# wo loaded over all 128 partitions, with o brought to the matching layout by eight selection matmuls

## Chip, cores and metric

One core of a Trainium2 chip. The metric is the device time of one execution in microseconds. The kernel before takes 357.08 us (median of 3 runs, 356.75 to 357.36; 357.03 with the fourth run that was made beside the changed kernel). All runs quoted here are of the fast state; runs of one kernel agree within about 0.3%. A profile is of one execution; its span, from the first to the last instruction, is about 2 us shorter than the time of that execution, and the same event can lie some tenths of a microsecond apart in two profiles.

## The reference

A decode step: one token for each of two batches. Attention with 32 heads over a cache of 4096 keys, a small dense branch, and a gate between them. PV below is the product of the softmax weights with V; o is its result.

```python
# x [2,1,512]; k_cache, v_cache [2,32,4096,128]; wq [512,4096]; wo [4096,512], all bf16
g = sigmoid((x * gate_w).sum(-1, keepdims=True))
q = (x @ wq) by heads
scores = einsum("bhqd,bhkd->bhqk", q, k) * 128 ** -0.5
o = einsum("bhqk,bhkd->bhqd", softmax(scores), v)
a = o.reshape(B, 1, 4096) @ wo
b = relu(x @ w1) @ w2
return g * a + (1 - g) * b
```

K and V are 67 MB each, the weights 11 MB. Nothing is used twice, so the work is mostly a stream from HBM.

## The kernel before

SyncE issues all large loads in one queue, in the order wq, w1, w2, 16 K tiles, 16 V tiles, wo, four 4 MB slots in SBUF being used in turn. K and V tiles cover all 128 partitions. wo (4 MB) goes into slot 0 as soon as the thirteenth V tile has been used (`pv_12`), and so stands behind the last three V tiles in the queue. Its rows are (head h, 32-row group c of 128/32 = 4, row r). Partition 32c + h holds the 32 rows r of (h, c), so one transfer serves one c and 32 partitions:

```python
wo_in = A_wo.rearrange("(h c r) n -> c h r n", c=4, r=32)
...
WO_CUTS = (0, 16, 24, 28, 30, 32)          # five chunks of r: half, a quarter, an eighth, ...
for k in range(5):
    lo, hi = WO_CUTS[k], WO_CUTS[k + 1]
    for c in range(4):
        load(f"ld_wo_{k}_{c}", wo_sb[32 * c:32 * c + 32, lo:hi, :], wo_in[c, :, lo:hi, :],
             waits=["pv_12"] if k + c == 0 else [], sem=f"wo{k}")
```

After the last V tile, o (64 rows (b, h), 128 columns d = 32c + r) is scaled and moved to that layout by eight small matmuls in four column tiles of the array, and then projected, chunk by chunk of wo:

```python
def o_spread():
    # on_sb[(b,h), d] = o * (gate / softmax sum)
    for b in range(2):
        for c in range(4):
            matmul(bank(MISC, 32 * b, 32, 32 * c, 32 * c + 32), lhsT=ident16[0:64, 32 * b:32 * b + 32],
                   rhs=on_sb[:, 32 * c:32 * c + 32], start=True, stop=True, tile_position=(0, 32 * c), ...)
    # os_sb[p, r, b] <- bank(MISC)
def proj():
    for r in range(32):
        for c in range(4):                 # here c is a block of 128 output columns
            # at r in WO_CUTS: wait for that chunk of wo
            matmul(acc(c), lhsT=os_sb[:, r, :], rhs=wo_sb[:, r, 128 * c:128 * c + 128], start=(r == 0), stop=(r == 31), ...)
```

Of the kernel before, what the change touches and what calls it, by code (L numbers as in the profile page):

```python
# [4 lines left out]
ALU = mybir.AluOpType  # L5
# [134 lines left out]
def bass_gated_mix__gqa_block_cached__dense_activation_relu__decode_kernel(  # L140
# [12 lines left out]
    P = _Prog(nc)  # L153
    f32, b16 = dt.float32, dt.bfloat16
    sb = nc.alloc_sbuf_tensor
# [3 lines left out]
    ident16 = sb("ident16", [128, 128], b16)  # L159
    eye32 = sb("eye32", [128, 32, 32], b16)  # L160
    dmask = sb("dmask", [128, 4], b16)
    row3 = sb("row3", [128, 4, 4, 4], f32)
    rmask = sb("rmask", [128, 4], f32)
    sst = sb("sst", [128, PER, 64], f32)
    selb = sb("selb", [128, 124], f32)
    zt = sb("zt", [128, 512], b16)
    x_sb = sb("x_sb", [2, 512], b16)
    gw_sb = sb("gw_sb", [1, 512], b16)
# [25 lines left out]
    on_sb = sb("on_sb", [64, 128], b16)  # L194
# [6 lines left out]
    wo_sb = kv_sb[:, 0, :, :].rearrange("p r d -> p (r d)").rearrange("p (r n) -> p r n", r=32)  # L201
# [4 lines left out]
    def bank(b, c0, n, p0=0, p1=128):  # L206
        return PSF[p0:p1, 512 * b + c0:512 * b + c0 + n]
# [7 lines left out]
    O_BANK, MISC, ACC = 6, 7, 0  # L215

    def acc(c):
        return bank(ACC, 0, 128, 32 * c, 32 * c + 2)
# [4 lines left out]
    w2a_in = B_w2[0:1280, :].rearrange("(p t) n -> p t n", p=128)  # L223
    w2b_in = B_w2[1280:1376, :]
    wq_in = A_wq.rearrange("(p t) n -> p t n", p=128)
    wo_in = A_wo.rearrange("(h c r) n -> c h r n", c=4, r=32)
    out_ap = out.rearrange("b s d -> (b s) d")

    def kv_in(n):
# [5 lines left out]
    def load(name, dst, src, waits=(), eng="sp", sem=None):  # L235
        P.add(eng, lambda e: e.dma_start(dst, src), waits=waits, signal=name, sem=sem or name, inc=16)  # L236
# [7 lines left out]
    for n in range(32):  # L244
        waits = [{2: "f", 3: "qT"}[n]] if n in (2, 3) else []
# [4 lines left out]
    WO_CUTS = (0, 16, 24, 28, 30, 32)  # L250
    for k in range(5):
        lo, hi = WO_CUTS[k], WO_CUTS[k + 1]
        for c in range(4):
            load(f"ld_wo_{k}_{c}", wo_sb[32 * c:32 * c + 32, lo:hi, :], wo_in[c, :, lo:hi, :], waits=["pv_12"] if k + c == 0 else [],
                 sem=f"wo{k}")


    P.add("pool", lambda e: e.memset(ident16[:], 0.0), signal="c_i0")
# [1 line left out]
                                            compare_op=ALU.not_equal, fill=1.0, base=0, channel_multiplier=1),  # L260
          waits=["c_i0"], signal="c_id")
    P.add("pool", lambda e: e.memset(eye32[:], 0.0), waits=["c_id"], signal="c_e0")
    P.add("pool", lambda e: e.affine_select(out=eye32[:], in_=eye32[:], pattern=[[1, 32], [-1, 32]],
                                            compare_op=ALU.not_equal, fill=1.0, base=0, channel_multiplier=0),
          waits=["c_e0"], signal="c_eye")
    P.add("pool", lambda e: e.memset(row3[:], 0.0), waits=["c_eye"], signal="c_r0")
    P.add("pool", lambda e: e.affine_select(out=row3[:], in_=row3[:], pattern=[[-32, 4], [-4, 4], [-1, 4]],
                                            compare_op=ALU.not_equal, fill=1.0, base=0, channel_multiplier=1),
          waits=["c_r0"], signal="c_row3")
    P.add("pool", lambda e: e.memset(dmask[:], 0.0), waits=["c_row3"], signal="c_d0")  # L270
    for q in range(4):
        P.add("pool", lambda e, q=q: e.memset(dmask[32 * q:32 * q + 32, q:q + 1], 1.0), waits=["c_d0"] if q == 0 else [],
              signal="c_d" if q == 3 else None)
# [7 lines left out]
    for k in range(4):  # L281
        P.add("pe", lambda e, k=k: e.matmul(bank(k, 0, 512), lhsT=zt[:, 0:128], rhs=zt[:, :], start=True, stop=True),
              waits=["c_zt"] if k == 0 else [])
    for t in range(4):
        P.add("pe", lambda e, t=t: e.transpose(bank16(4, 2 * t, 2), x_sb[0:2, t:512:4], ident16[0:2, 0:2]),
              waits=["c_id", "ld_x"] if t == 0 else [], signal="xT" if t == 3 else None)
    for t in range(4):
        P.add("pe", lambda e, t=t: e.transpose(bank16(5, 2 * t, 1), gw_sb[0:1, t:512:4], ident16[0:1, 0:1]),  # L288
              waits=["ld_gw"] if t == 0 else [], signal="gwT" if t == 3 else None)
    P.add("dve", lambda e: e.tensor_copy(out=xT_sb[:, :, :], in_=bank16(4, 0, 8).rearrange("p (t b) -> p t b", t=4)),  # L290
          waits=["xT"], signal="xT_sb")
    P.add("dve", lambda e: e.tensor_copy(out=gwb_sb[:, :, :],
                                         in_=PSB[:, 5120:5128:2].unsqueeze(2).to_broadcast([128, 4, 128])),
          waits=["gwT"], signal="gwb")
    for t in range(4):
        P.add("pe", lambda e, t=t: e.matmul(bank(6, 0, 2), lhsT=gwb_sb[:, t, :], rhs=xT_sb[:, t, :],
                                            start=(t == 0), stop=(t == 3)),
              waits=["xT_sb", "gwb"] if t == 0 else [], signal="logit" if t == 3 else None)
    P.add("act", lambda e: e.activation(out=g_sb[:, :], in_=bank(6, 0, 2), func=ACT.Sigmoid), waits=["logit"], signal="g")
    P.add("dve", lambda e: e.tensor_scalar(out=gm_sb[:, :], in0=g_sb[:, :], scalar1=-1.0, scalar2=1.0, op0=ALU.mult, op1=ALU.add),  # L300
          waits=["g"], signal="gm")
    for h in range(HQ):
        for t in range(4):
            P.add("pe", lambda e, h=h, t=t: e.matmul(bank(7, 2 * h, 2), lhsT=wq_sb[:, t, h * 128:(h + 1) * 128],  # L304
                                                     rhs=xT_sb[:, t, :], start=(t == 0), stop=(t == 3)),
                  waits=["ld_wq"] if h + t == 0 else [], signal="qT" if h == HQ - 1 and t == 3 else None)
# [213 lines left out]
    def o_spread():  # L520
        P.add("dve", lambda e: e.tensor_scalar(out=on_sb[:, :], in0=bank(O_BANK, 0, 128, 0, 64), scalar1=rg[:, 0:1], scalar2=None,
                                               op0=ALU.mult), waits=["ov_15", "rg_0", "rg_1"], signal="on")
        for b in range(2):
            for c in range(4):
                P.add("pe", lambda e, b=b, c=c: e.matmul(
                    bank(MISC, 32 * b, 32, 32 * c, 32 * c + 32), lhsT=ident16[0:64, 32 * b:32 * b + 32],
                    rhs=on_sb[:, 32 * c:32 * c + 32], start=True, stop=True, tile_position=(0, 32 * c), skip_group_check=True),
                    waits=["on"] if b + c == 0 else [], signal="os" if (b, c) == (1, 3) else None)
        P.add("dve", lambda e: e.tensor_copy(out=os_sb[:, :, :].rearrange("p r b -> p b r"),
                                             in_=bank(MISC, 0, 64).rearrange("p (b r) -> p b r", b=2)),  # L530
              waits=["os"], signal="os_sb")

    def proj():
        for r in range(32):
            for c in range(4):
                w = ["os_sb"] if r == 0 else []
                if r in WO_CUTS:
                    w = w + [f"ld_wo_{WO_CUTS.index(r)}_{k}" for k in range(4)]
                P.add("pe", lambda e, r=r, c=c: e.matmul(acc(c), lhsT=os_sb[:, r, :], rhs=wo_sb[:, r, 128 * c:128 * c + 128],  # L539
                                                         start=(r == 0), stop=(r == 31), tile_position=(0, 32 * c), skip_group_check=True),  # L540
                      waits=w if c == 0 else [], signal="proj" if (r, c) == (31, 3) else None)
# [27 lines left out]
    for p in range(PER):  # L569
        v_sum(p, NIT - 1)  # L570
    stage_s()
    o_spread()
    proj()
    P.add("dve", lambda e: e.tensor_tensor(out=out_sb[:, :], in0=bank(ACC, 0, 128, 0, 98), in1=f_sb[:, :], op=ALU.add),  # L574
          waits=["proj"], signal="res")
    for b, eng in enumerate(("sp", "act")):
        P.add(eng, lambda e, b=b: e.dma_start(out_ap[b].rearrange("(c n) -> c n", c=4), out_sb[b:97 + b:32, :]), waits=["res"],
              signal=f"st_{b}", sem="st", inc=16)
# [51 lines left out]
```

## Time and profile before

| | before |
|---|---|
| time, median | 357.08 us |
| profiled span | 354.7 us |
| DMA rate while V loads | 433 GB/s |
| DMA rate while wo loads | 207 to 231 GB/s |
| start of the last PV batch (32 matmuls on the last V tile) | 334.99 us |
| end of the projection | 352.02 us |

Read it as one long transfer with a tail. As long as the loads set the end, time at which the DMA runs below its own best rate is lost, whatever "busy" says. The prediction below shows the lines. In them PE is TensorE (PEld its weight loads), DVE VectorE, ACT ScalarE, POOL GpSimd and SP SyncE. A stretch has its bounds, its length, the busy microseconds of PE, PEld, DVE, ACT and POOL with the number of instructions, then the granted TensorE clock (1.00 is full speed), the mean busy share of the 16 DMA engines, and GB/s. L478 is PV, L525 the selection of o, L529 the copy to os_sb, L539 the projection, L574 the final add; the change moves these to L481, L528, L532, L542, L577.

### The profile page before, as it was taken

What the parts mean: (1) busy time and instruction counts of PE and PEld (TensorE: products, weight loads), DVE (VectorE), ACT (ScalarE), POOL (GpSimd) and SP (SyncE); (2) the same over time, 40 slices, a digit from 0 to 9 for tenths busy, and PEclk for the clock granted to TensorE, in tenths of its full rate; (3) what the DMA queues carried; (4) which work ended last, traced back from release to release, by engine and by line L of the source; (5) the groups of instructions that cost most, each with busy time, mean ns of one, the idle gap of its engine ahead of it and who ended that gap; (6) DMA issues with size and microseconds to landing.
All of it is one profiled execution on the core that took longest, in us unless ns stands there. A gap on an engine that the chain in (4) does not pass through costs nothing.

```text
span 354.7 us, 8320 instructions
## 1 busy us (share of the span) xinstructions
PE 232.1 (65%) x3475; PEld 159.0 (45%) x3476; DVE 150.7 (42%) x285; ACT 99.9 (28%) x105; POOL 24.0 (7%) x47
## 2 busy tenths in 40 slices
PE   2535999999999999999993534444333344444242
PEld 0525887788777877788881111111111111111021
DVE  1012667666667666677669642111222222111020
ACT  1002666566565665576664000000000000000000
POOL 4030100111111111100000000000000000000000
PEclk9999999999999999999998586666555666555565
DMA  9999999999999999999999999999999999999994
GB/s 355 389 453 418 416 450 428 416 434 440 418 432 436 432 425 436 440 421 440 440 418 432 436 430 423 432 440 425 432 443 421 432 443 425 421 432 443 248 218 106
DMA packets 6146, 145.61 MB, mean 411 GB/s; under 512 B 915, under 2 KB 1014, under 8 KB 1398
## 3 DMA queue, kind: packets, MB, share of 16 engines
q1 hardware_dynamic: 6120, 145.43, 98.2%
q8 instruction: 9, 0.15, 0.2%
q14 instruction: 3, 0.02, 0.0%
q10 hardware_dynamic: 14, 0.00, 0.0%
HBM read 145.43 MB, written 0.00 MB: 410 GB/s over the span
## 4 chain that ended last, share of the span: by engine, by line
DMA 78%; PE 15%; SPq 3%; DVE 2%; issue 1%; DVEq 0%
DMA kv_sb<-in_A_k_cache_dram 35%; DMA kv_sb<-in_A_v_cache_dram 28%; DMA kv_sb<-in_A_wo_dram 10%; PE PS L353 8%; DMA kv_sb<-in_B_w_dram 5%; PE PS L478 4%; SPq L236 3%; PE PS L365 2%; DVE mt L419 1%; PE PS L330 0%; DVE ET_sb L432 0%; DVE pst L462 0%; DVE mT L421 0%; PE PS L539 0%; DVE mx L422 0%
## 5 line engine op out<-in xcount | busy, mean ns | idle before, releaser
L389 DVE COPY kt_sb<-PS 128x1024 bf16<-128x1024 bf16 x160 | 105.6, 688 | 58.4 <-PE PS L353 58.3
L353 PE MATMUL PS<-ident,kv_sb 128*128 128x128 bf16 x2048 | 122.9, 221 | 10.8 <-DMA kv_sb<-in_A_k_cache_dram 9.8
L353 PEld LDWEIGHTS PS<-ident,kv_sb 128*128 128x128 bf16 x2048 | 116.3, 99 | 25.0 <-issue 16.6
L386 ACT ACTIVATE kt_sb<-PS 128x1024 bf16<-128x1024 bf16 x96 | 94.5, 1022 | 72.4 <-PE PS L353 72.4
L478 PE MATMUL PS<-kv_sb,pst 128*16 128x512 bf16 x512 | 55.2, 608 | 59.8 <-issue 42.8
L478 PEld LDWEIGHTS PS<-kv_sb,pst 128*16 128x16 bf16 x512 | 16.5, 122 | 89.9 <-issue 89.2
L490 DVE TENSOR_SCALAR vo<-PS,rmask 128x128 f32<-128x128 f32 x16 | 5.6, 351 | 109.8 <-PE PS L478 109.8
L365 PE MATMUL PS<-kt_sb,qst 128*32 128x512 bf16 x512 | 34.2, 382 | 1.1 <-DVE kt_sb L389 1.1
L505 PE MATMUL PS<-vo,sst 128*64 128x128 f32 x32 | 8.4, 352 | 29.0 <-DVE vo L491 29.0
L399 POOL TENSOR_TENSOR qst<-q_sb,eye 128x512 bf16 x16 | 16.5, 1040 | 128.2 <-PE PS L365 116.5
L505 PEld LDWEIGHTS PS<-vo,sst 128*64 128x64 f32 x32 | 3.7, 165 | 42.5 <-issue 30.2
L491 DVE SCALAR_TENSOR_TENSOR vo<-PS,rmask,vo 128x128 f32<-128x128 f32 x48 | 16.8, 351 | 1.7
L365 PEld LDWEIGHTS PS<-kt_sb,qst 128*32 128x32 bf16 x512 | 10.9, 95 | 12.7 <-issue 3.3
L513 POOL COPY sst<-selb 128x64 f32 x16 | 3.6, 236 | 146.0 <-PE PS L505 146.0
L462 DVE TENSOR_TENSOR pst<-ET_sb,dmask 128x512 bf16<-128x512 bf16 x16 | 10.8, 684 | 0.1
L539 PE MATMUL PS<-kv_sb,os_sb 128*2 128x128 bf16 x128 | 4.3, 305 | 6.5 <-DMA kv_sb<-in_A_wo_dram 6.5
L539 PEld LDWEIGHTS PS<-kv_sb,os_sb 128*2 128x2 bf16 x128 | 2.9, 112 | 7.7 <-DMA kv_sb<-in_A_wo_dram 4.7
L304 PE MATMUL PS<-xT_sb,kv_sb 128*128 128x2 bf16 x128 | 3.6, 165 | 3.6 <-DMA kv_sb<-in_A_wq_dram 3.6
L304 PEld LDWEIGHTS PS<-xT_sb,kv_sb 128*128 128x128 bf16 x128 | 3.5, 104 | 3.7 <-DMA kv_sb<-in_A_wq_dram 3.7
L574 DVE TENSOR_TENSOR out_sb<-PS,f_sb 98x128 bf16<-98x128 f32 x1 | 0.3, 292 | 10.5 <-PE PS L539 10.5
L288 PE MATMUL PS<-ident,gw_sb 1*128 1x1 bf16 x4 | 0.3, 172 | 4.6 <-DMA gw_sb<-in_gate_w_dram 4.6
L307 DVE TENSOR_SCALAR q_sb<-PS 128x64 bf16<-128x64 f32 x1 | 0.2, 224 | 6.8 <-PE PS L304 6.8
(62 smaller groups left out, 35.9 us busy)
## 6 DMA issues: line engine op xcount, KB each, us to landing
kv_sb<-in_A_k_cache_dram SPq DMA_DIRECT2D x16, 4096.0 KB, 29.2
kv_sb<-in_A_v_cache_dram SPq DMA_DIRECT2D x16, 4096.0 KB, 35.1
kv_sb<-in_A_wq_dram SPq DMA_DIRECT2D x1, 4096.0 KB, 12.1
kv_sb<-in_A_wo_dram SPq DMA_DIRECT2D x4, 512.0 KB, 32.0
kv_sb<-in_B_w_dram SPq DMA_DIRECT2D x1, 1376.0 KB, 14.9
kv_sb<-in_B_w_dram SPq DMA_DIRECT2D x1, 1280.0 KB, 19.1
kv_sb<-in_A_wo_dram SPq DMA_DIRECT2D x4, 256.0 KB, 36.2
kv_sb<-in_A_wo_dram SPq DMA_DIRECT2D x4, 128.0 KB, 37.3
```

The source lines that it names most:

```text
L236: P.add(eng, lambda e: e.dma_start(dst, src), waits=waits, signal=name, sem=sem or name, inc=16)
L304: P.add("pe", lambda e, h=h, t=t: e.matmul(bank(7, 2 * h, 2), lhsT=wq_sb[:, t, h * 128:(h + 1) * 128], rhs=xT_sb[:, t, :], start=(t == 0), ...
L353: P.add("pe", lambda e, iv, q=q, rr=rr: e.transpose(bank16(4 + q % 4, rr * 128, 128), kv_sb[:, p, 64 * e_ + 8 * q + rr, :], ident16[:, :]) ...
L365: P.add("pe", lambda e, iv, c=c, h=h: e.matmul(bank(2 * (p % 2) + e_, 0, 512, 32 * h, 32 * h + 32), lhsT=qst[:, p, h, c, :], rhs=kt_sb[:, ...
L386: P.add("act", lambda e, iv, dst=dst, src=src: e.activation(out=dst, in_=src, func=ACT.Copy), waits=waits, signal=signal, sem=f"ev{u}{q}")
L389: P.add("dve", lambda e, iv, dst=dst, src=src: e.tensor_copy(out=dst, in_=src), waits=waits, signal=signal, sem=f"ev{u}{q}")
L399: P.add("pool", lambda e, iv, p=p: e.tensor_tensor(out=qst[:, p, :, :, :], in0=q_sb[:, p % 2, bass.ds(iv * 8 + 4 * (p // 2), 4)].unsqueeze ...
L462: return e.tensor_tensor(out=pst[:, p, :, :].rearrange("p k (c h) -> p k c h", h=4), in0=ET_sb[:, p % 2, :, bass.ds(k0, 4)].unsqueeze(3).t ...
L478: P.add("pe", lambda e, iv, j=j, r0=r0: e.matmul(bank(4 + p % 2, 0, 512, 32 * (j % 4), 32 * (j % 4) + 16), lhsT=pst[:, p, j, :], rhs=kv_sb ...
L491: return e.scalar_tensor_tensor(out=dst, in0=src, scalar=rmask[:, c:c + 1], in1=dst, op0=ALU.mult, op1=ALU.add)
L505: P.add("pe", lambda e, iv: e.matmul(bank(O_BANK, 0, 128, 0, 64), lhsT=sst[:, p, :], rhs=vo[:, p % 2, :], start=False, stop=True, skip_gro ...
L539: P.add("pe", lambda e, r=r, c=c: e.matmul(acc(c), lhsT=os_sb[:, r, :], rhs=wo_sb[:, r, 128 * c:128 * c + 128], start=(r == 0), stop=(r == ...
```

## The change

Its intent: give each transfer of wo all 128 partitions, as K and V have them, so that it is written as fast as they are (V 433 GB/s, wo 207 to 231). Partition p = 4h + c now holds rows 32p to 32p + 31 of wo, which is how wo lies in memory. o must follow: a constant `spread` with ones at column 4k + 3 of row k is used in eight windows as the stationary operand, so that row (b, h) goes to partition 4h + c; four matmuls accumulate for each b.

```diff
--- before.py
+++ after.py
@@ -163,6 +163,7 @@
     rmask = sb("rmask", [128, 4], f32)
     sst = sb("sst", [128, PER, 64], f32)
     selb = sb("selb", [128, 124], f32)
+    spread = sb("spread", [64, 260], b16)
     zt = sb("zt", [128, 512], b16)
     x_sb = sb("x_sb", [2, 512], b16)
     gw_sb = sb("gw_sb", [1, 512], b16)
@@ -223,7 +224,7 @@
     w2a_in = B_w2[0:1280, :].rearrange("(p t) n -> p t n", p=128)
     w2b_in = B_w2[1280:1376, :]
     wq_in = A_wq.rearrange("(p t) n -> p t n", p=128)
-    wo_in = A_wo.rearrange("(h c r) n -> c h r n", c=4, r=32)
+    wo_in = A_wo.rearrange("(p r) n -> p r n", p=128)
     out_ap = out.rearrange("b s d -> (b s) d")
 
     def kv_in(n):
@@ -250,9 +251,7 @@
     WO_CUTS = (0, 16, 24, 28, 30, 32)
     for k in range(5):
         lo, hi = WO_CUTS[k], WO_CUTS[k + 1]
-        for c in range(4):
-            load(f"ld_wo_{k}_{c}", wo_sb[32 * c:32 * c + 32, lo:hi, :], wo_in[c, :, lo:hi, :], waits=["pv_12"] if k + c == 0 else [],
-                 sem=f"wo{k}")
+        load(f"ld_wo_{k}", wo_sb[:, lo:hi, :], wo_in[:, lo:hi, :], waits=["pv_12"] if k == 0 else [])
 
 
     P.add("pool", lambda e: e.memset(ident16[:], 0.0), signal="c_i0")
@@ -267,7 +266,11 @@
     P.add("pool", lambda e: e.affine_select(out=row3[:], in_=row3[:], pattern=[[-32, 4], [-4, 4], [-1, 4]],
                                             compare_op=ALU.not_equal, fill=1.0, base=0, channel_multiplier=1),
           waits=["c_r0"], signal="c_row3")
-    P.add("pool", lambda e: e.memset(dmask[:], 0.0), waits=["c_row3"], signal="c_d0")
+    P.add("pool", lambda e: e.memset(spread[:], 0.0), waits=["c_row3"], signal="c_s0")
+    P.add("pool", lambda e: e.affine_select(out=spread[:], in_=spread[:], pattern=[[-1, 260]],
+                                            compare_op=ALU.not_equal, fill=1.0, base=3, channel_multiplier=4),
+          waits=["c_s0"], signal="c_spr")
+    P.add("pool", lambda e: e.memset(dmask[:], 0.0), waits=["c_spr"], signal="c_d0")
     for q in range(4):
         P.add("pool", lambda e, q=q: e.memset(dmask[32 * q:32 * q + 32, q:q + 1], 1.0), waits=["c_d0"] if q == 0 else [],
               signal="c_d" if q == 3 else None)
@@ -523,9 +526,9 @@
         for b in range(2):
             for c in range(4):
                 P.add("pe", lambda e, b=b, c=c: e.matmul(
-                    bank(MISC, 32 * b, 32, 32 * c, 32 * c + 32), lhsT=ident16[0:64, 32 * b:32 * b + 32],
-                    rhs=on_sb[:, 32 * c:32 * c + 32], start=True, stop=True, tile_position=(0, 32 * c), skip_group_check=True),
-                    waits=["on"] if b + c == 0 else [], signal="os" if (b, c) == (1, 3) else None)
+                    bank(MISC, 32 * b, 32), lhsT=spread[:, 128 * b + 3 - c:128 * b + 131 - c], rhs=on_sb[:, 32 * c:32 * c + 32],
+                    start=(c == 0), stop=(c == 3)),
+                    waits=["on", "c_spr"] if b + c == 0 else [], signal="os" if (b, c) == (1, 3) else None)
         P.add("dve", lambda e: e.tensor_copy(out=os_sb[:, :, :].rearrange("p r b -> p b r"),
                                              in_=bank(MISC, 0, 64).rearrange("p (b r) -> p b r", b=2)),
               waits=["os"], signal="os_sb")
@@ -535,7 +538,7 @@
             for c in range(4):
                 w = ["os_sb"] if r == 0 else []
                 if r in WO_CUTS:
-                    w = w + [f"ld_wo_{WO_CUTS.index(r)}_{k}" for k in range(4)]
+                    w = w + [f"ld_wo_{WO_CUTS.index(r)}"]
                 P.add("pe", lambda e, r=r, c=c: e.matmul(acc(c), lhsT=os_sb[:, r, :], rhs=wo_sb[:, r, 128 * c:128 * c + 128],
                                                          start=(r == 0), stop=(r == 31), tile_position=(0, 32 * c), skip_group_check=True),
                       waits=w if c == 0 else [], signal="proj" if (r, c) == (31, 3) else None)
```

## The prediction

> **What bounds the kernel now.** I read the picture by slices first, to see which resource is full and when it stops being so. Columns are 40 slices of 354.7/40 = 8.87 us.
>
> ```profile
> PE   2535999999999999999993534444333344444242
> PEclk9999999999999999999998586666555666555565
> DMA  9999999999999999999999999999999999999994
> GB/s 355 389 453 418 416 450 428 416 434 440 418 432 436 432 425 436 440 421 440 440 418 432 436 430 423 432 440 425 432 443 421 432 443 425 421 432 443 248 218 106
> ```
>
> The DMA engines are busy from end to end, so bytes per microsecond set the time. But the rate stays between 416 and 453 GB/s only up to slice 37; then it falls to 248, 218 and 106 while "busy" stays at nine tenths. Busy engines at half the rate are engines that wait for something. Next I cut the tail into stretches (columns after the engines' busy times: granted clock, DMA share, GB/s).
>
> ```profile
> 320.00:325.00 5.00, 2.44 (x24) 0.91 (x28) 0.00 (x0) 0.00 (x0) 0.00 (x0) 0.50 1.01 433
> 325.00:330.00 5.00, 1.80 (x14) 0.44 (x6) 1.40 (x4) 0.00 (x0) 0.00 (x0) 0.50 0.99 413
> 330.00:335.00 5.00, 0.01 (x2) 0.04 (x3) 0.00 (x0) 0.00 (x0) 0.00 (x0) 0.50 1.00 216
> 340.00:345.00 5.00, 1.47 (x46) 1.18 (x50) 0.65 (x3) 0.00 (x0) 0.00 (x0) 0.67 0.94 207
> 345.00:350.00 5.00, 2.29 (x84) 1.71 (x76) 0.00 (x0) 0.00 (x0) 0.00 (x0) 0.50 0.87 218
> ```
>
> The break is at 330 us and complete: 433 before, about 215 after. Third, what runs there and what it waits for: the timeline of the tail (start, duration, engine, line, what, idle before and its releaser).
>
> ```profile
> 322.56 3.59 PE L478 MATMUL PS<-kv_sb,pst 128*16 128x512 bf16 x32 [3.75 <-issue]
> 334.99 3.52 PE L478 MATMUL PS<-kv_sb,pst 128*16 128x512 bf16 x32 [6.49 <-issue]
> 340.66 0.34 DVE L521 TENSOR_SCALAR on_sb<-PS,rg 64x128 bf16<-64x128 f32 x1 [0.59 <-PE PS L505]
> 341.06 0.22 PE L525 MATMUL PS<-on_sb,ident 64*32 64x32 bf16 x8 [0.44 <-DVE on_sb L521]
> 341.34 0.23 DVE L529 CAST os_sb<-PS 128x64 bf16<-128x64 f32 x1 [0.34 <-PE PS L525]
> 344.16 1.88 PE L539 MATMUL PS<-kv_sb,os_sb 128*2 128x128 bf16 x64 [2.88 <-DMA kv_sb<-in_A_wo_dram]
> 348.25 1.02 PE L539 MATMUL PS<-kv_sb,os_sb 128*2 128x128 bf16 x32 [2.22 <-DMA kv_sb<-in_A_wo_dram]
> 351.61 0.38 PE L539 MATMUL PS<-kv_sb,os_sb 128*2 128x128 bf16 x8 [0.64 <-DMA kv_sb<-in_A_wo_dram]
> 352.04 0.29 DVE L574 TENSOR_TENSOR out_sb<-PS,f_sb 98x128 bf16<-98x128 f32 x1 [10.47 <-PE PS L539]
> ```
>
> The last V tile is multiplied at 334.99. Then o is normalised and respread by 341.57, and the projection has to wait for wo chunk by chunk; its last eight matmuls start when the last chunk lands, at about 351.6. The chain of waits says the same:
>
> ```profile
> 315.51 36.05 DMA kv_sb<-in_A_wo_dram
> 351.56 0.04 issue
> 351.61 0.41 PE PS L539 x8
> ```
>
> Those 36 us are queueing, not transfer: 20 wo issues stand behind three V tiles. Only the part after V, some 20 us, is wo moving: 4.19 MB at about 215 GB/s.
>
> [...] Today each wo transfer covers 32 partitions; V covers 128. [...] 207 to 218 in the tail, 433 for V. [...]
>
> **The change, part by part.**
>
> *1. The wo stream.* Twenty transfers of 32 partitions become five of 128 with the same bytes and the same run lengths per partition (16 KB down to 2 KB). Written like V, wo should move at V's rate: 4.19 MB / 433 GB/s = 9.7 us, instead of about 20.
>
> *2. The last V tile.* PV batches start every 9.7 us (293.41, 303.16, 312.85, 322.56), except the last: 12.4 us later. I read the extra 2.7 us as wo: engines that finish V early start the first wo block[...]. [...] the last V lands at 322.56 + 9.7 = 332.3.
>
> *3. Landing of wo.* Counting on from there at 433 GB/s, half of wo (chunk 0) lands at 337.1, three quarters at 339.6, seven eighths at 340.8, fifteen sixteenths at 341.4, all at **342.0**. A second count: the one-microsecond stretches from 329 to 351 sum to 4.67 MB; at 433 that takes 10.8 us, so the last byte moves at 339.8, and with the 1.2 us between last bytes and last landing seen before (350.4 to 351.6) it lands at 341.0. I take 341 to 342.
>
> *4. The compute path beside it.* From the start of the last PV to the end of the os_sb copy: 341.57 - 334.99 = 6.58 us, now from 332.3: 338.9. The selection matmuls are on this path. Before, eight small ones ran in four column tiles in 0.22 us. Now eight have 128-column weights and use the whole array, one after another. The wq matmuls (L304, 128 columns, 2 moving columns) took 3.57 us for 128, 28 ns each at clock 1.00, so 56 ns at the clock of 0.50 that rules most of the tail: 8 x 56 = 0.45 us plus one pipeline of 0.17 us = 0.6 us; I add 0.3 us. os_sb is ready at **339.2**.
>
> *5. The projection.* 128 matmuls, whose first 64 took 1.88 us at clock 0.50: (1.88 - 0.31)/63 = 25 ns each. All 128 need 128 x 0.025 + 0.3 = 3.5 us, with some 0.1 us for the chunk waits. From 339.2 it ends at **342.8**. wo's last landing plus its eight matmuls gives 342.0 + 0.4 = 342.4. So both tails end nearly together, and compute is a little later: of the 9.6 us that wo lands earlier, about 0.4 is not collected.
>
> *6. What moves elsewhere.* SyncE issues 5 instead of 20 wo transfers (it issued from 306.79 for 11.4 us); wo is served only from 330, so this is worth nothing. GpSimd gets one memset and one select of 260 columns, some 0.3 + 0.5 us by the rows for 128 and 1024 columns (select 0.30 and 1.27); they delay dmask from 5.4 to about 6.2 us, and GpSimd's next work starts at 17.02. Worth nothing.
>
> *Sum.* The projection ended at 352.02 and now at 342.8: 9.2 us. The final add and store after it stay. 357.08 - 9.2 = **347.9 us**, 2.6% faster.
>
> **Rivals.** (a) [...] The before layout reads wo at a pitch of 128 KB between partitions, and runs get short. Short runs are not it: the first half of wo, in 16 KB runs, is already at 216. A bad pitch would be cured too, as the new layout reads at V's pitch of 32 KB. If the short runs did count after all, the last half of wo might take 7 us instead of 4.9: about 350. (b) *The bound moves to TensorE and VectorE.* This happens in my sum. If the last V tile still landed at 335, os_sb would be at 341.9, the projection would end at 345.5 and the time would be 350.6, within 2%. Against it: nothing but wo is queued behind V. (c) *The tail is hidden anyway.* Then nothing changes, some 357.4 with the slower selection. The 10.47 us idle of VectorE and the waits of L539 for wo speak against it. (d) *TensorE gets a full clock in the shorter tail*: [...] wo's landing sets the end, and if that is 341.0 the time is 346.5.
>
> **Range and chances.** Centre 347.9. Below, (d) gives 346.5 and a little less; above, (a) and (b) give 350 to 350.6. The line for 2% is 349.9. I put 346.0 to 350.4 at eight in ten. Faster by over 2%: 0.84[...]; within 2%: 0.15; slower: 0.01.
>
> **What would show it.** Right: the rate stays above 400 GB/s until about 339; the last PV starts near 332.3; the L525 group takes 0.4 to 0.7 us; L539 runs its 128 matmuls with at most short waits for wo, ending near 342.8. Step 1 is wrong if the rate still halves; step 2 if the last PV starts near 335; step 4 if L525 takes over 1 us; step 5 if L539 still waits over 1 us for wo. The prediction fails if wo, alone in the queue, doesn't reach V's rate, or V comes late for another reason.

## The result and the profile after

The changed kernel takes 348.01 us (median of 4 runs, 347.38 to 348.74) beside 357.03 us before. The ratio is 0.9748, interval 0.9725 to 0.977: 2.5% faster. A ratio is the mean time of one kernel's fast runs over that of the other's in the same rounds, so not quite the ratio of the medians quoted.

First the slices of the changed kernel; a slice is now 8.65 us.

```profile
DMA  8999999999999999999999999999999999999994
GB/s 315 424 433 422 422 435 430 435 426 428 432 432 428 432 443 432 428 428 435 428 428 435 435 433 428 426 435 428 435 428 435 435 428 428 435 432 432 432 405 165
```

The three low slices at the end have become one: 405, and a last slice of 165 that is partly empty. "Busy" looks the same as before; only the GB/s line tells the two kernels apart. The same tail in stretches:

```profile
325.00:330.00 5.00, 2.06 (x18) 0.50 (x10) 1.40 (x4) 0.00 (x0) 0.00 (x0) 0.79 0.99 426
330.00:335.00 5.00, 2.22 (x24) 0.91 (x28) 0.00 (x0) 0.00 (x0) 0.00 (x0) 0.55 0.95 405
335.00:340.00 5.00, 2.53 (x34) 0.87 (x30) 1.98 (x6) 0.00 (x0) 0.00 (x0) 0.50 0.98 403
340.00:345.00 5.00, 3.47 (x128) 3.18 (x120) 0.29 (x1) 0.00 (x0) 0.00 (x0) 0.58 0.23 87
```

At 330, where the old kernel broke to 216, there is now 405. Third, the timeline of the tail:

```profile
323.07 3.59 PE L481 MATMUL PS<-kv_sb,pst 128*16 128x512 bf16 x32 [4.01 <-issue]
332.78 3.59 PE L481 MATMUL PS<-kv_sb,pst 128*16 128x512 bf16 x32 [4.01 <-issue]
...
339.17 0.39 PE L528 MATMUL PS<-on_sb,spread 64*128 64x32 bf16 x8 [0.44 <-DVE on_sb L524]
339.60 0.23 DVE L532 CAST os_sb<-PS 128x64 bf16<-128x64 f32 x1 [0.49 <-PE PS L528]
339.89 3.58 PE L542 MATMUL PS<-kv_sb,os_sb 128*2 128x128 bf16 x128 [0.32 <-DVE os_sb L532]
343.52 0.29 DVE L577 TENSOR_TENSOR out_sb<-PS,f_sb 98x128 bf16<-98x128 f32 x1 [3.69 <-PE PS L542]
```

The last PV batch follows the one before by 9.71 us, about the spacing of those before it (9.68 to 9.76). All 128 projection matmuls run as one group. Its releaser is os_sb, not a DMA: wo is never waited for. Before, the group was in five pieces with a wo wait before each.

### The profile page after: what moved, and what is told of

Same layout as the page of the kernel before. It is cut to its first block, busy times and chain, and to the rows that moved or that the text cites. A ratio compares the mean times of both kernels' runs of the same rounds, so it can differ in the third digit from the quotient of the medians.

```text
span 346.1 us, 8309 instructions
## 1 busy us (share of the span) xinstructions
PE 231.6 (67%) x3475; PEld 160.6 (46%) x3476; DVE 150.5 (43%) x285; ACT 100.0 (29%) x105; POOL 24.8 (7%) x49
## 4 chain that ended last, share of the span: by engine, by line
DMA 62%; PE 28%; issue 5%; DVE 4%; SPq 1%; DVEq 0%
DMA kv_sb<-in_A_k_cache_dram 33%; DMA kv_sb<-in_A_v_cache_dram 29%; PE PS L356 16%; PE PS L481 7%; PE PS L368 4%; DVE vo L494 1%; PE PS L542 1%; DVE mt L422 1%; PE PS L508 1%; SPq L237 1%; DVE vo L493 0%; DVE ET_sb L435 0%; DVE pst L465 0%; DVE mT L424 0%; PE PS L528 0%
## 5 line engine op out<-in xcount | busy, mean ns | idle before, releaser
L508 PE MATMUL PS<-vo,sst 128*64 128x128 f32 x32 | 8.4, 352 | 29.1 <-DVE vo L494 29.1
L508 PEld LDWEIGHTS PS<-vo,sst 128*64 128x64 f32 x32 | 3.7, 165 | 41.9 <-issue 29.9
L542 PE MATMUL PS<-kv_sb,os_sb 128*2 128x128 bf16 x128 | 3.6, 310 | 0.3 <-DVE os_sb L532 0.3
```

What stands on the lines that cost most here:

```text
L508: P.add("pe", lambda e, iv: e.matmul(bank(O_BANK, 0, 128, 0, 64), lhsT=sst[:, p, :], rhs=vo[:, p % 2, :], start=False, stop=True, skip_gro ...
L542: P.add("pe", lambda e, r=r, c=c: e.matmul(acc(c), lhsT=os_sb[:, r, :], rhs=wo_sb[:, r, 128 * c:128 * c + 128], start=(r == 0), stop=(r == ...
```

## The experiments

Twelve kernels ran; all results are correct but that of e9, which is wrong on purpose. "Before" was run beside each and took 356.7 to 356.9 us in these jobs. My theory, an estimate from V's 433 GB/s with 128 partitions and wo's 207 to 231 with 32: the half rate came from the destination partitions of a single transfer. Rivals: the source pitch (the distance in HBM between the data of neighbouring partitions), the number of transfers, the number of engines, and the path of compute. Short diffs are against the changed kernel unless said otherwise; where a chunk is cut, the projection waits for all its parts.

### e1: the new layout in blocks of 32 partitions

```diff
-        load(f"ld_wo_{k}", wo_sb[:, lo:hi, :], wo_in[:, lo:hi, :], ...)
+        for c in range(4):
+            p0, p1 = 32 * c, 32 * c + 32
+            load(f"ld_wo_{k}_{c}", wo_sb[p0:p1, lo:hi, :], wo_in[p0:p1, lo:hi, :], ..., sem=f"wo{k}")
```

> The changed kernel with its source layout (partition pitch 32 KB) and its selection matmuls kept, but each wo chunk written by four transfers of 32 partitions each, 20 in all. Theory (only the number of destination partitions of one transfer matters): the rate falls to about 215 GB/s once V is done, the last PV batch starts near 335 us instead of 332.8, wo lands near 351.5 and the time is 357 us (356.5 to 358), the whole gain gone. Rival (the old source pitch of 128 KB was what halved the rate): the time stays at 348 us and the rate above 400 GB/s.

Measured 356.94 us, ratio to before 1.0004 (0.9995 to 1.0013). Stretches of e1:

```profile
325.00:330.00 5.00, 1.27 (x14) 0.35 (x6) 1.41 (x4) 0.00 (x0) 0.00 (x0) 0.84 1.02 429
330.00:335.00 5.00, 0.29 (x4) 0.14 (x8) 0.00 (x0) 0.00 (x0) 0.00 (x0) 0.50 1.01 220
335.00:340.00 5.00, 3.30 (x32) 0.98 (x25) 1.40 (x4) 0.00 (x0) 0.00 (x0) 0.60 0.97 221
```

The whole gain is gone, with the new source pitch, row order and selection still in place: 220 and 221 GB/s from 330 to 340, where the changed kernel has 405 and 403. The rival that the new source pitch brought the gain has fallen. (Whether the old pitch would be slow by itself, in transfers of 128 partitions with sixteen packets in flight, no run tests.) The four PV matmuls in the second line show the late V tile again: it starts at 334.70.

### e2: 20 transfers, each over 128 partitions

```diff
-        load(f"ld_wo_{k}", wo_sb[:, lo:hi, :], wo_in[:, lo:hi, :], ...)
+        step = (hi - lo + 3) // 4 if k else 2
+        for j, r0 in enumerate(range(lo, hi, step)):
+            load(f"ld_wo_{k}_{j}", wo_sb[:, r0:r0 + step, :], wo_in[:, r0:r0 + step, :], ..., sem=f"wo{k}")
```

> The changed kernel with each wo chunk cut by rows into several transfers that each cover all 128 partitions, 20 in all, as many as before the change, with runs of 2 KB and 1 KB. Theory (partitions, not the number of transfers): 348 us, at most 349 us, tail rate above 390 GB/s, last PV start near 332.8. Rival (the gain came from issuing 5 transfers in place of 20, a fixed cost of some 9.0/15 = 0.6 us each): 357 us.

Measured 348.46 us, ratio 0.9767 (0.9751 to 0.9784). A stretch of e2:

```profile
330.00:335.00 5.00, 2.59 (x28) 1.00 (x32) 0.00 (x0) 0.00 (x0) 0.00 (x0) 0.50 1.01 380
```

The number of transfers is not what mattered. The short runs cost a little rate: 380 GB/s here and 379 from 335 to 340, where the changed kernel has 405 and 403, so my 390 was a little high. (In the packet records of the trace a 2 KB packet of e2 takes a median 87 ns; sixteen at once, as the DMA share of 1.01 has it, make 377 GB/s, so the run length accounts for it.) Here the last chunks do arrive after TensorE wants them (waits of 0.33, 0.29 and 0.36 us in the timeline).

### e3: the old layout in one transfer for each chunk

Against the kernel before; the small selection matmuls stay.

```diff
-        for c in range(4):
-            load(f"ld_wo_{k}_{c}", wo_sb[32 * c:32 * c + 32, lo:hi, :], wo_in[c, :, lo:hi, :], ...)
+        load(f"ld_wo_{k}", wo_sb[:, lo:hi, :], wo_in[:, :, lo:hi, :], ...)
```

> The kernel before, in its old layout and with its old small selection matmuls, but one transfer per chunk over all 128 partitions, whose source pattern has c (4 values) as its slowest dimension. Theory A (destination partitions alone decide): 348 us without any change of layout. Theory B [...]: only four engines carry wo, DMA share about 0.25 in the tail, [...] wo takes about 39 us and the time is about 376 us (370 to 382).

Measured 386.99 us, ratio 1.0828. Two stretches of e3, columns as above:

```profile
340.00:345.00 5.00, 0.00 (x0) 0.00 (x0) 0.00 (x0) 0.00 (x0) 0.00 (x0) 0.50 0.26 88
350.00:355.00 5.00, 0.00 (x0) 0.00 (x0) 0.00 (x0) 0.00 (x0) 0.00 (x0) 0.50 0.27 95
```

A share of a quarter fits four working engines of 16, as theory B has it, and the packet records show four packets in flight (below). So 128 destination partitions are not enough either. The source of e3 has c, of size 4, as its slowest dimension; that this is why four engines work was theory B's guess, and no run varies c alone to show it. To merge the transfers in the old layout costs 30 us (387 beside 357): this is why the change altered wo's layout, and o's with it. The size was off: 376 expected, 387 measured. The 39 us expected for wo are those of 4.19 MB at a quarter of V's 433 GB/s, 108; the four engines moved 84 to 95 GB/s from 335 to 360.

### e4: the two halves from two queues

Against the kernel before: blocks c = 2 and 3 are issued from the ACT queue when the last V tile has landed.

```diff
-        for c in range(4):
+        for c in range(2):
             load(f"ld_wo_{k}_{c}", ...)
+    def wo_odd():                    # ACT's program, ahead of o_spread()
+        for k in range(5):
+            for c in (2, 3):
+                load(f"ld_wo_{k}_{c}", ..., waits=["pv_12", "ld_kv_31"] if (k, c) == (0, 2) else [], eng="act", sem=f"wo{k}b")
```

> The kernel before with its 32-partition transfers, but the blocks of partitions 64 to 127 are issued from the ACT queue once the last V tile has landed, those of 0 to 63 from the SP queue as before. Theory [...]: about 357 us, tail rate still near 220 GB/s. Rival ([...] both halves are written at once): tail rate well over 300 GB/s and 349 to 352 us; the last PV start stays near 335 in both, since the first block is still behind V on the SP queue.

Measured 358.77 us, ratio 1.0041 (1.0027 to 1.0056). Stretches of e4:

```profile
335.00:340.00 5.00, 3.16 (x32) 1.06 (x32) 0.00 (x0) 0.00 (x0) 0.00 (x0) 0.50 1.04 210
340.00:345.00 5.00, 1.32 (x15) 0.42 (x10) 1.98 (x6) 0.00 (x0) 0.00 (x0) 0.50 1.00 214
```

ACT could only begin at 336.8, as V was later still (last PV at 336.84). But SyncE's half alone, 2.1 MB begun after 330 at 210 GB/s, lasts until 340 at least, so from 337 to 340 both queues had work and the rate did not rise (210 GB/s from 335 to 340). The rival has fallen for this arrangement.

### e5: 32 partitions in steps of four

```diff
+        for c in range(4):
+            ps = slice(c, c + 125, 4)
+            load(f"ld_wo_{k}_{c}", wo_sb[ps, lo:hi, :], wo_in[ps, lo:hi, :], ..., sem=f"wo{k}")
```

> As e1 (four transfers of 32 partitions per chunk, changed layout), but each transfer takes every fourth partition (c, c+4, ... c+124) in place of a block. [...] Theory A [...]: full rate, 348 to 349 us. Theory B [...]: still about half the rate, near 357 us[...].

Measured 347.84 us, ratio 0.9746 (0.9729 to 0.9764). Stretches of e5:

```profile
330.00:335.00 5.00, 2.56 (x28) 0.95 (x32) 0.00 (x0) 0.00 (x0) 0.00 (x0) 0.50 0.99 419
335.00:340.00 5.00, 2.54 (x62) 1.30 (x58) 1.98 (x6) 0.00 (x0) 0.00 (x0) 0.84 0.97 396
```

As many transfers and partitions as e1, and the rate of the changed kernel: 419 and 396 GB/s, where that has 405 and 403, and e1 has 220 and 221. So it was neither the number of partitions nor one transfer for all: what counts is which partitions a transfer takes. Theory A, the full rate, held; theory B, about half of it, fell. Which engine writes which partition is not on record, so why these partitions do better is not shown.

### e11: the control, 32 partitions in steps of two within one half

```diff
+        for c in range(4):
+            p0 = 64 * (c // 2) + c % 2
+            load(f"ld_wo_{k}_{c}", wo_sb[p0:p0 + 63:2, lo:hi, :], wo_in[p0:p0 + 63:2, lo:hi, :], ..., sem=f"wo{k}")
```

> The control for e5: four transfers of 32 partitions per chunk again, but every second partition of one half (0, 2, ... 62; 1, 3, ... 63; 64, ...; 65, ...). [...] Theory [...]: 357 us, tail rate near 218 GB/s. Rival (a partition stride in itself[...] made e5 fast): 348 us.

Measured 356.7 us, ratio 0.9998 (0.9989 to 1.0007). Stretches of e11:

```profile
330.00:335.00 5.00, 0.00 (x0) 0.00 (x0) 0.00 (x0) 0.00 (x0) 0.00 (x0) 0.50 1.02 216
335.00:340.00 5.00, 3.50 (x32) 1.06 (x32) 0.70 (x2) 0.00 (x0) 0.00 (x0) 0.60 1.00 224
```

Up to 350 it stays at 217 and 224 GB/s. A stride in itself brought nothing here: steps of two within a half (partitions 0 to 63 or 64 to 127) have 216 to 224 GB/s, the blocks of e1 219 to 225.

### e6: blocks of 64 partitions

```diff
+        for c in range(2):
+            p0, p1 = 64 * c, 64 * c + 64
+            load(f"ld_wo_{k}_{c}", wo_sb[p0:p1, lo:hi, :], wo_in[p0:p1, lo:hi, :], ..., sem=f"wo{k}")
```

> As e1, but two transfers of 64 partitions per chunk (0 to 63, 64 to 127), ten in all. Theory [...]: as slow as e1, 357 us, tail rate about 218 GB/s. Rival (rate grows with the number of partitions in a transfer): about three quarters of the way, 350 to 352 us, tail rate over 300 GB/s.

Measured 356.5 us, ratio 0.999 (0.9982 to 0.9997); 206 to 223 GB/s from 330 to 350. 64 partitions of one half are as slow as 32 (e1: 219 to 225).

### e12: the blocks of e1 in another order

```diff
+        for c in (0, 2, 1, 3):       # the rest as in e1
```

> e1 with its four blocks of 32 partitions in the order 0-31, 64-95, 32-63, 96-127, so that successive transfers go to the two halves [...] in turn. Theory [...]: 357 us, tail rate about 218 GB/s. Rival [...]: tail rate over 300 GB/s, 349 to 353 us.

Measured 354.82 us, ratio 0.9951 (0.9934 to 0.9967). Stretches of e12:

```profile
330.00:335.00 5.00, 0.33 (x4) 0.14 (x8) 0.00 (x0) 0.00 (x0) 0.00 (x0) 0.50 1.00 236
335.00:340.00 5.00, 3.29 (x33) 1.08 (x26) 1.40 (x4) 0.00 (x0) 0.00 (x0) 0.71 1.00 241
340.00:345.00 5.00, 2.51 (x74) 1.91 (x73) 0.57 (x2) 0.00 (x0) 0.00 (x0) 0.63 0.96 249
```

Neither expectation was met. The mean of these stretches is 242 GB/s, that of the same ones in e1 222: 9% more, 2 us. Taking the blocks from the two halves in turn brought this much and no more; what it is due to is not shown.

### e7 and e8: half of wo wide, half in blocks

```diff
+        split = k > 0                # e7; in e8: split = k == 0
+        for c in range(4 if split else 1):
+            p0, p1 = (32 * c, 32 * c + 32) if split else (0, 128)
+            load(f"ld_wo_{k}_{c}", wo_sb[p0:p1, lo:hi, :], wo_in[p0:p1, lo:hi, :], ..., sem=f"wo{k}")
```

> The changed kernel with chunk 0 (half of wo) still one transfer of 128 partitions, chunks 1 to 4 as blocks of 32. My theory of step 2 [...]: V is undisturbed, last PV start near 332.8; half of wo at about 218 GB/s instead of 432 costs 9.6 - 4.85 = 4.8 us, so wo lands near 347.4 and the time is about 352.4 us (351.5 to 353.2). If V is late for another reason whenever blocks are in the queue: last PV start near 335.

> The mirror of e7: chunk 0 as four blocks of 32 partitions, chunks 1 to 4 as transfers of 128. Step 2 says: the last PV starts about 2.3 to 2.7 us late, near 335, as in the kernel before. The wo stream as a whole loses the same 4.8 us as in e7, and as the compute path (335 + 6.8 = 341.8, then 3.5) ends at 345.3, before wo, the time is the same as in e7, about 352.4 us (351.5 to 353.2). If the late V were worth time by itself, e8 would be 2 us slower than e7.

Measured: e7 351.88 us (ratio 0.9854, 0.9837 to 0.987), e8 354.12 us (ratio 0.9922, 0.9905 to 0.9938). Timelines, e7 and then e8, of the last PV and the first two groups of the projection:

```profile
332.51 3.59 PE L484 MATMUL PS<-kv_sb,pst 128*16 128x512 bf16 x32 [4.01 <-issue]
...
339.63 1.88 PE L546 MATMUL PS<-kv_sb,os_sb 128*2 128x128 bf16 x64 [0.32 <-DVE os_sb L535]
343.54 1.02 PE L546 MATMUL PS<-kv_sb,os_sb 128*2 128x128 bf16 x32 [2.04 <-DMA kv_sb<-in_A_wo_dram]
```

```profile
334.63 3.18 PE L484 MATMUL PS<-kv_sb,pst 128*16 128x512 bf16 x32 [6.04 <-issue]
...
343.85 1.88 PE L546 MATMUL PS<-kv_sb,os_sb 128*2 128x128 bf16 x64 [3.13 <-DMA kv_sb<-in_A_wo_dram]
346.06 1.02 PE L546 MATMUL PS<-kv_sb,os_sb 128*2 128x128 bf16 x32 [0.33 <-DMA kv_sb<-in_A_wo_dram]
```

e7 met its expectation. The late V is shown to come from the blocks directly behind it: on time with the wide chunk there, 2.1 us late with the blocks. But e8 is 1.7 us over its expectation, and the criterion I had set ("2 us slower than e7: the late V is worth time by itself") would be met. The timeline speaks against that reading: os_sb was ready at 341 and the projection still waited 3.13 us for chunk 0. The excess is in the DMA. By the one-microsecond stretches the half rate lasted from 331 to 343, 12 us and 2.39 MB, of which 2.10 MB are blocks: some 0.3 MB of V was written at half rate too (the packet records below show nine slow V packets of 32 KB, 0.29 MB), and the rate averaged 199 GB/s against some 230 in e7's slow stage. 12 us less the 9.6 planned and the 0.7 us that those 0.3 MB take at 432 is 1.7 us. That a changeover from blocks to other work costs about this is read from the profile and not isolated by a run.

### e9: half of wo not loaded

```diff
-        load(f"ld_wo_{k}", ...)
+        if k == 0: load(f"ld_wo_{k}", ...)
```

> Wrong result on purpose: the changed kernel without the loads of chunks 1 to 4 (2.1 MB less, ending some 4.9 us earlier); the projection reads old data there and does the same 128 matmuls. If the compute path sets the end, as the profile after shows (its projection never waits for wo), the time stays within 0.5 us of the changed kernel's 348.0. If the landing of wo still sets part of the end, it falls by 1 us or more, down to about 346.

Measured 347.91 us, ratio 0.9745 (0.9732 to 0.9758), as the changed kernel's 0.9748 in its own job. The timeline of e9 has the same last group:

```profile
339.58 3.58 PE L543 MATMUL PS<-kv_sb,os_sb 128*2 128x128 bf16 x128 [0.33 <-DVE os_sb L533]
```

2.1 MB less to load is worth nothing that these runs resolve: compute sets the end now.

### e10: the selection matmuls four times

```diff
-        for b in range(2):
+        for b in (0, 1) * 4:
```

> The changed kernel with its eight selection matmuls done four times over (32, the same result). They took 0.39 us for 8 in the profile after. If they are on the path that sets the end, 24 more at (0.39 - 0.19)/7 = 29 ns each cost 0.7 us: 348.7 us; at the 56 ns of my prediction 1.3 us: 349.3 us. If wo's landing sets the end instead and has slack, 348.0 to 348.3 us.

Measured 348.12 us, ratio 0.9759 (0.9745 to 0.9772): 0.2 us over e9 in the same job, and the intervals overlap. The timeline of e10:

```profile
338.82 1.00 PE L530 MATMUL PS<-on_sb,spread 64*128 64x32 bf16 x32 [0.44 <-DVE on_sb L524]
...
340.15 3.13 PE L544 MATMUL PS<-kv_sb,os_sb 128*2 128x128 bf16 x128 [0.32 <-DVE os_sb L534]
```

24 more matmuls take (1.00 - 0.39)/24 = 25 ns each, 0.6 us in all, and the projection has to wait for them, with no wait for wo. The clock was not the same for the 32: it was 1.00 until about 339.2 and then 0.50. In this execution the projection took 3.13 us instead of 3.58, at a higher granted clock (0.74 against 0.58 from 340 to 345). Such swings of the clock are as large as the effect, so the time doesn't decide between 0.2 and 0.7 us; the 0.6 us is the trace's number, and my 1.3 us is ruled out.

No experiment beat the changed kernel by more than the noise. e5 equals it with 20 transfers.

### The packets themselves

The kept traces also hold the size, start and duration of every DMA packet, which the views do not list. Read directly, they settle three points.

*What "busy" hid.* Half of wo moves in packets of 16 KB. Their median duration was 1.18 us in the kernel before, e1 and e11, 1.22 us in e6 and 1.09 us in e12, but 0.61 us in the changed kernel and in e5. About sixteen were in flight all the while in either case (e1 from 337 to 347, the changed kernel from 333 to 340). So the time was lost within each packet, not between them. In e5 none of the 93 packets that began between 332 and 337 took over 0.63 us, so none showed the half rate of theory B.

*The late V.* V moves in packets of 32 KB, which take 1.22 us. In the kernel before, nine of them began after the first packet of wo, and these took 2.16 us (median); the nine of e8 took 2.14 us. In the changed kernel and in e7 nine began after wo as well, and took 1.21 us. The last V packet ended at 333.1 in e8 and 332.0 in e7: this is 1.1 of the 2.1 us by which V is late. The other microsecond lies between that end and the start of PV (1.5 us in e8, 0.6 us in e7); what holds it is not shown.

*The four engines of e3.* From 340 to 360 four packets were in flight for 97% of the time. Of its 16 KB packets about a third took over 0.9 us, up to 1.25 us, the others 0.61 us: this is where 108 GB/s became 84 to 95. Why a third was slowed is not shown.

## Why the prediction was right

347.9 us was predicted, 348.01 measured. By its steps:

| step | predicted | measured |
|---|---|---|
| 1. rate of wo | V's, 433 GB/s | 405, 403 from 330 to 340 |
| 2. start of the last PV | 332.3 | 332.78 |
| 3. wo all landed | 341 to 342 | not waited for; last bytes between 342 and 343 |
| 4. added by the new selection | 0.3 us | 0.39 - 0.22 = 0.17 us |
| 4. last PV to os_sb ready | 6.9 us | 339.83 - 332.78 = 7.05 us |
| 4. os_sb ready | 339.2 | 339.83 |
| 5. projection, one run | 3.6 us | 3.58 us |
| 5. end of the projection | 342.8 | 343.5 |
| 6. GpSimd's constants | 0.8 us, hidden | 0.31 + 0.40 us, hidden: its next work at 17.20 |

*Steps 1 and 2* are the cause, and the experiments show it by undoing them alone: e1 loses everything, e2 keeps nearly everything, and e7 against e8 ties the late V (2.1 us) to the blocks behind it; the packets show V itself slowed there (2.14 us in place of 1.21), which explains 1.1 us of the delay. That V would come on time with the new layout was an estimate from the spacing of the batches before it, 9.7 us; it came 9.71 us after the one before. Rival (a) fell with e1 for the pitch, and short runs cost little: e2 is 0.4 us above the changed kernel by the medians of two jobs, which is within their noise. Rival (c) fell with the gain itself.

*Step 3* was about a microsecond early: the rate was somewhat below V's up to 340, and then 254 and 162 GB/s in the last two microseconds, as engines ran out of work (DMA share 0.65 and 0.42). This did not reach the end, because *steps 4 and 5* held: the end had passed to TensorE and VectorE, as the missing wait and e9 show. Rival (b) in its mild form is thus what happened; in its strong form, with V still late, it did not. Rival (d) did not come in this profile: the clock was 0.50 throughout the projection.

*Sizes.* The last PV is 0.5 us later than predicted because every PV batch of this profile is (303.67 against 303.16 four batches from the end); e2 and e9 start it at 332.4 and 332.5. Selection was mis-sized: I took the spacing of 28 ns at full clock and doubled it for a clock of 0.50. Its eight matmuls ran at a clock of 0.50 (339.1 to 339.6) with (0.39 - 0.18)/7 = 29 ns between them, so the spacing did not double, and 0.3 us should have been 0.17. (My own numbers, 0.6 less 0.22, would even have given 0.4.) The rest of the path was too short: I took it over from a profile in which the two L505 matmuls had run at full clock in 0.40 us, and here, as L508, they took 0.66 us at a clock of 0.50. These errors offset each other only in part: the profiled projection ended 8.5 us earlier, not 9.2, and the profiled runs differ by 356.77 - 348.3 = 8.5 us. The medians differ by 9.0. So the closeness of 347.9 to 348.01 is partly luck within half a microsecond.

*Slips in the reading.* The prediction gives the tail 207 to 218 GB/s. The stretch from 335 to 340, which it does not show, has 231. And it puts all slices up to the 37th between 416 and 453 GB/s, but the first two have 355 and 389. Neither changes a step.

*Where the reasoning was too narrow.* It treated "all 128 partitions" as the condition. e5 shows that 32 partitions do as well if chosen in steps of four (419 and 396 GB/s), and e3 that 128 do much worse when only four packets are in flight (84 to 95 GB/s). What I could not settle is why the 32 partitions of e5, from both halves within one transfer, reach this rate, when the neighbouring transfers of e12, on different halves, have 242 GB/s.

## What to carry to other kernels

Look at GB/s beside DMA busy. Here a DMA share of 0.87 to 1.04 went with 207 to 231 GB/s in the kernel before and one of 0.95 and 0.98 with 405 and 403 in the changed one, and the cure was in which partitions each transfer takes (e5 beside e1), not in how many transfers there are (e2, 380 GB/s with 20). When transfers are merged, look at the DMA share as well: in e3 it fell to 0.26, and 30 us were lost. And when a transfer at the end gets faster, work out where the compute path ends: here it took over after a gain of 9 us, and with half of wo not loaded at all (e9) nothing more was gained.
